# Two attention branches on one core: x in sixteen turned pieces, one run of dummy products, three buffers for a polynomial tile, and a new written-out order

## The chip, the core and the metric

The kernel runs on one core of a Trainium2 chip. The metric is device time in microseconds (us) of one execution; the median of several runs is given. The engines are TensorE (PE, with its weight loads as PEld), ScalarE (ACT), VectorE (DVE), GpSimd (POOL) and SyncE (SP, which here issues most of the transfers).

## The reference

Two branches work on inputs of 2048 rows by 1024 columns, with 32 heads of width 32, in bfloat16. Their results are put side by side.

```python
# branch A: plain attention
qkv = (x @ wqkv).reshape(B, S, 3, H, Dh)
p = softmax(q @ k.T * Dh ** -0.5)
a = (p @ v) @ wo

# branch B: four segments of 512 rows, causal inside a segment, with a memory M, z
for s in range(4):
    p = softmax(qs @ ks.T * scale + mask)
    a_dot = p @ vs
    a_mem = (phi(qs) @ M) / (phi(qs) @ z + 1e-06)
    o = g * a_mem + (1.0 - g) * a_dot        # g = sigmoid(beta)
    M = M + phi(ks).T @ vs
    z = z + phi(ks).sum(over the rows)
b = concat(o) @ wo
return concatenate([a, b], axis=-1)
```

`phi(t)` is `t + 1` where t is positive and `exp(t)` elsewhere.

## The kernel before

**Tiles.** Four heads make a group (eight groups, `g` or `j`). A unit of branch A is one group and 256 queries, a column `c` of eight; a unit of branch B is a pair of groups in one segment. A unit is worked in sets: TensorE forms the logits of 128 keys for four heads ("row products", line 1169), ScalarE takes the exponential of 128 by 1024 of them at a time (line 1262) into a ring `P` of 20 buffers, and TensorE multiplies the result with V (line 1375) and with ones (line 1382), the latter for the sum of the softmax. DVE and POOL normalize (`turned`, line 1489 and on). Projections, output products and the memory of branch B are jobs that run between: eight groups of four products, nearly all issued by one helper (`mm4`, line 808).

**The polynomial.** In every unit of branch A after the first group's split parts, four key tiles send one head's tile around ScalarE: DVE reads the logits into `Y` (line 1210), POOL squares them into `Z` (line 1219) and writes a parabola into `Pc` (line 1220). The rings `Y`, `Z` and `Pc` have 3, 2 and 2 buffers. The exponential and the parabola hold for small logits; a guard computes a bound from squared norms (`square`, `guard_cols`, line 1613, `guard_end`, line 1668) and sets a bias and a flag (lines 1685 and 1693), on which ScalarE branches to a guarded version. A few numbers that the guards leave lie in the small tiles `cols`, `bias`, `braw` and `fp`.

**The head.** Before the first exponentials, branch A's x is loaded and turned on the way, by transposing transfers on SyncE's queue (`turn`, line 1547), in the pieces that `X_PIECES` lists: quarter of the rows, first and last block of 128 columns, and two times for the planner. The weights of group 0 (`W_A`) and half of those for V (`Wv_A`) are issued on ScalarE's own queue, ahead of and around the load of its table (line 1042). TensorE begins with products on a zeroed tile (`warm`, on `sqB`), in three runs of 7, 6 and 3 groups: at the start, behind the first two products of the first quarter, and at that quarter's end. `quarter` forms K and Q of one quarter of the rows; their copies (lines 1761 and 1763) and squares (line 1596) lead to the first two exponentials, which run without a guard, to the first bound (line 1306 makes good what it finds), to six guarded exponentials (line 1240), to the second bound, which rests on the second quarter, and to a correction factor (line 1646).

**The order.** Nothing is scheduled on the chip. A program simulates the engines with costs of its own, spreads the jobs evenly between release and due times (`level`, `plan_jobs`), and writes a fixed queue for each engine (`schedule`). `rearrange` then moves single entries as `MOVES` tells: "12+3" steps 12 on and pulls the entry three places behind to this one. Each engine takes its queue in order and waits on semaphores. `BANKS` says which of two accumulator banks each job or accumulation uses. In `emit`, an instruction of ACT, DVE or POOL that must come after a near one on its own engine is made to wait for it.

Of the kernel before, what the change touches and what calls it, by code (L numbers as in the profile page):

```python
# [6 lines left out]
dt = mybir.dt  # L7
ACT = mybir.ActivationFunctionType
# [18 lines left out]
    "667676677676667666667666766676666666667676677676666676666676666666676766776766676666676666667676766776766667666666767667"  # L27
    "767666766666766667666766677666666667677676767666667666766666666676767667676667666666676676677676666676666766666667766776"
    "766667666667666766667666667666666666766767767676677666666667676776766666766666667677676766676666667676776766676667666766"
    "67666676666666676666766"  # L30
# [3 lines left out]
Y_RING, Z_RING, C_RING = 3, 2, 2  # L34
# [9 lines left out]
CUBIC = [[0, 2, 4, 6], [0, 2, 4, 6], [0, 2, 4, 6], [0, 2, 4, 6], [0, 2, 4, 6], [0, 2, 4, 6], [0, 2, 4, 6], [0, 2, 4, 6], [0, 2, 4, 6], [0, 2, 4, 6], [0, 2, 4, 6], [0, 2, 4, 6], [0, 2, 4, 6], [0, 2, 4, 6], [0, 2, 4, 6], [0, 2, 4, 6]]  # L44
# [9 lines left out]
BIAS_PART = (17, 16, 18)  # L54
PARTS = ((0, 0), (0, 1), (1, 0), (1, 1), (1, 2), (1, 3), (2, 0), (2, 1), (2, 2), (2, 3))
WARM = (7, 6, 3)
X_PIECES = ((0, 0, 2, 0.7, 3.8), (0, 2, 4, 0.7, 5.8), (0, 4, 6, 2.2, 4.5), (0, 6, 8, 2.2, 2.9), (1, 0, 4, 2.6, 3.0),
            (1, 4, 8, 2.5, 3.0), (2, 0, 8, 4.4, 3.5), (3, 0, 8, 4.9, 3.5))
# [85 lines left out]
class Op:  # L144
# [17 lines left out]
    def __hash__(self):  # L162
# [4 lines left out]
SWITCH = 0.10  # L167
AHEAD_OF_GUARD = 2
# [607 lines left out]
class _Kernel:  # L776
# [925 lines left out]
    def plan_prologue(self):  # L1702
# [8 lines left out]
        def warm(key, n, dur, behind=None):  # L1711
            for _ in range(n):
                o = self.pe(lambda e: self.mm4(e, self.ps[:, 512 * 5:512 * 6], dummy[:, 0:P], dummy[:, :], True, True), dur, key,
                            [rd], [self.bank[5]])
                if behind:
                    o.order.add(behind)
# [530 lines left out]
```

## Time and profile before

| | us |
|---|---|
| median of three runs (lowest, highest) | 1068.11 (1067.42, 1068.65) |
| the profiled execution | 1067.08 |
| its span | 1065.3 |
| busy: PE, ACT, POOL, DVE | 1025.6, 1001.1, 723.5, 710.7 |

The span runs from the first to the last instruction of the profiled execution; what lies outside it makes the rest of that execution's own time. Views of the profile give times in us from the span's start, and shapes as partitions by elements. A bracket at the end of a line of the order of time holds the idle time of the engine just before, and what ended it. In a group's line the busy time stands behind the bar, and the idle time before its instructions behind the next.

### The profile page before, as it was taken

What the parts mean: (1) busy time and instruction counts of PE and PEld (TensorE: products, weight loads), DVE (VectorE), ACT (ScalarE), POOL (GpSimd) and SP (SyncE); (2) the same over time, 40 slices, a digit from 0 to 9 for tenths busy, and PEclk for the clock granted to TensorE, in tenths of its full rate; (3) what the DMA queues carried; (4) which work ended last, traced back from release to release, by engine and by line L of the source; (5) the groups of instructions that cost most, each with busy time, mean ns of one, the idle gap of its engine ahead of it and who ended that gap; (6) DMA issues with size and microseconds to landing.
All of it is one profiled execution on the core that took longest, in us unless ns stands there. A gap on an engine that the chain in (4) does not pass through costs nothing.

```text
span 1065.3 us, 55407 instructions
## 1 busy us (share of the span) xinstructions
PE 1025.6 (96%) x25276; PEld 554.2 (52%) x25276; DVE 710.7 (67%) x1452; ACT 1001.1 (94%) x1193; POOL 723.5 (68%) x999
## 2 busy tenths in 40 slices
PE   8999999999999999999999998999999999999998
PEld 4556555566554454556555454466545544445554
DVE  2446677765666878787656888778556887674544
ACT  4999999999999999998999999899999899999996
POOL 1005578667776897888867897897756777885552
PEclk9999999999999999999999999999999999999999
DMA  9013261016121530034321322044131750122101
GB/s 205 17 43 92 67 140 25 15 19 142 30 78 50 134 84 18 3 60 101 89 78 48 76 55 48 10 91 81 38 84 50 194 143 3 37 67 77 33 23 58
DMA packets 171547, 72.01 MB, mean 68 GB/s; under 512 B 135216, under 2 KB 169520, under 8 KB 171312
## 3 DMA queue, kind: packets, MB, share of 16 engines
q1 hardware_dynamic: 167904, 67.40, 26.2%
q8 instruction: 199, 3.26, 1.3%
q10 hardware_dynamic: 3408, 1.05, 0.5%
q14 instruction: 36, 0.29, 0.1%
HBM read 45.23 MB, written 11.67 MB: 53 GB/s over the span
## 4 chain that ended last, share of the span: by engine, by line
PE 60%; ACT 31%; DVE 6%; issue 1%; DMA 1%; POOL 1%; SPq 1%; ACTq 0%; DVEq 0%; POOLq 0%
ACT P L1262 30%; PE ps L808 30%; PE ps L1169 12%; PE ps L1375 9%; PE ps L1382 8%; PE ps L1836 1%; DVE Y L1210 1%; DVE T L1489 1%; DMA xT_A<-in_A_x_dram 1%; DVE KQ_B L1583 1%; SPq L1547 1%; ACT P L1240 0%; DVE PKQ_B L1895 0%; POOL Z L1219 0%; PE ps L1613 0%
## 5 line engine op out<-in xcount | busy, mean ns | idle before, releaser
L1262 ACT ACTIVATE P<-ps 128x1024 bf16<-128x1024 f32 (+1 forms) x1178 | 991.0, 996 | 40.6 <-PE ps L1169 25.1
L1219 POOL TENSOR_TENSOR Z<-Y 128x512 f32<-128x512 f32 x287 | 304.6, 1066 | 202.9 <-DVE Y L1210 181.9
L1382 PE MATMUL ps<-P,onesb 128*32 128x256 bf16 (+1 forms) x4386 | 300.6, 270 | 0.0
L1375 PE MATMUL ps<-P,V_A 128*32 128x256 bf16 x3618 | 256.8, 274 | 0.7 <-DVE V_A L1846 0.3
L1210 DVE TENSOR_SCALAR Y<-ps 128x512 f32<-128x512 f32 x239 | 163.6, 685 | 117.7 <-PE ps L1169 107.1
L1169 PE MATMUL ps<-KQ_A 32*128 32x256 bf16 x4096 | 204.4, 272 | 15.4 <-ACT P L1262 9.5
L1220 POOL TENSOR_SCALAR Pc<-Z 128x512 bf16<-128x512 f32 x239 | 156.2, 657 | 23.1 <-PE ps L1382 6.3
L1169 PEld LDWEIGHTS ps<-KQ_A 32*128 32x128 bf16 x4096 | 62.8, 92 | 168.5 <-ACT P L1262 114.4
L808 PE MATMUL ps<-xT_A,W_A 128*32 128x512 bf16 (+1 forms) x2184 | 142.0, 369 | 3.1 <-DMA xT_A<-in_A_x_dram 2.6
L1382 PEld LDWEIGHTS ps<-P,onesb 128*32 128x32 bf16 x4386 | 128.6, 96 | 27.9 <-issue 11.3
L808 PE MATMUL ps<-xT_B,W_B 128*32 128x512 bf16 (+1 forms) x2160 | 137.8, 370 | 1.5 <-DVE gc L1792 0.6
L1375 PEld LDWEIGHTS ps<-P,V_A 128*32 128x32 bf16 x3618 | 107.7, 96 | 32.8 <-issue 14.7
L1382 PE MATMUL ps<-Pc,onesb 128*32 128x256 bf16 x478 | 123.1, 273 | 0.0
L1375 PE MATMUL ps<-Pc,V_A 128*32 128x256 bf16 x478 | 122.3, 274 | 0.4 <-POOL Pc L1220 0.2
L1291 POOL TENSOR_SCALAR_AFFINE_SELECT P<-P 128x768 bf16<-128x768 bf16 (+1 forms) x96 | 75.3, 800 | 34.6 <-ACT P L1262 33.9
L1489 DVE STREAM_TRANSPOSE T<-ps 128x512 f32<-128x512 f32 x122 | 86.6, 710 | 16.2 <-PE ps L1382 12.6
L808 PEld LDWEIGHTS ps<-xT_A,W_A 128*32 128x32 bf16 x2184 | 52.4, 96 | 49.1 <-issue 18.9
L808 PEld LDWEIGHTS ps<-xT_B,W_B 128*32 128x32 bf16 x2160 | 51.6, 96 | 46.5 <-issue 19.3
L808 PE MATMUL ps<-Wo_B,OT_B 128*32 128x512 bf16 (+1 forms) x1072 | 71.6, 371 | 0.1
L808 PE MATMUL ps<-Wv_B,xT_B 128*32 128x512 bf16 (+1 forms) x1076 | 68.8, 371 | 0.1
L1583 DVE CAST KQ_A<-ps 128x512 bf16<-128x512 f32 x60 | 41.1, 685 | 37.7 <-PE ps L808 37.0
L1583 DVE CAST outsb<-ps 128x512 bf16<-128x512 f32 x56 | 38.7, 690 | 33.2 <-PE ps L1375 17.1
(107 smaller groups left out, 1207.6 us busy)
## 6 DMA issues: line engine op xcount, KB each, us to landing
Wv_B<-in_B_wv_dram SPq DMA_DIRECT2D x32, 256.0 KB, 3.7
W_B<-in_B_wk_dram SPq DMA_DIRECT2D x32, 256.0 KB, 3.8
W_B<-in_B_wq_dram SPq DMA_DIRECT2D x32, 256.0 KB, 4.3
Wo_B<-in_B_wo_dram SPq DMA_DIRECT2D x32, 256.0 KB, 3.2
out_dram<-outsb SPq DMA_DIRECT2D x56, 128.0 KB, 1.9
W_A<-in_A_wqkv_dram SPq DMA_DIRECT2D x14, 256.0 KB, 4.3
ot_a_scratch<-OTst SPq DMA_DIRECT2D x50, 64.0 KB, 1.8
xT_A<-ot_a_scratch SPq DMA_DIRECT2D x6, 512.0 KB, 4.6
```

What stands on the lines that cost most here:

```text
L808: ins = e.matmul(out[r], w[:, r], x, start=start, stop=stop, tile_position=(0, 32 * t), skip_group_check=True)
L1169: ins = e.matmul(out, kap, qap, start=st, stop=True, tile_position=(32 * h, 0), skip_group_check=True)
L1210: o = self.dve(lambda e: e.tensor_scalar(Y[:, :], src, SCALE, MID, ALU.mult, ALU.add), 512, key - 9.0, [self.bank[bank]], [rY], fixed=0.15)
L1219: self.pool(lambda e: e.tensor_tensor(Z[:, :], Y[:, :], Y[:, :], ALU.mult), 512, key, [rY], [rZ], rate=0.58)
L1220: return self.pool(lambda e: e.tensor_scalar(dst, Z[:, :], C2, REST, ALU.mult, ALU.add), 512, key, [rZ], [rP], rate=TS_RATE)
L1262: a = self.act(guarded if early and not free else lambda e: e.activation(dst, src, ACT.Exp, scale=SCALE), cols, key, rd, wr, fixed=EXP_FIXED)
L1291: self.pool(lambda e: e.affine_select(v, v, pattern=pat, compare_op=ALU.is_ge, fill=0.0, base=0, channel_multiplier=-1), 2 * nd * P, key + ...
L1375: ins = e.matmul(self.ps[32 * h:32 * h + 32, 512 * obk + q0:512 * obk + q0 + nq], v, p, start=first, stop=last, tile_position=(0, 32 * h), ...
L1382: ins = e.matmul(self.ps[32 * h:32 * h + 32, lcol + q0:lcol + q0 + nq], self.onesb[:, 0:32], p, start=False, stop=last, tile_position=(0, ...
L1489: self.dve(lambda e: e.transpose(T2[:, :], src), 512, k - NORM_K, [obk.res], [ro, rl], fixed=0.17)
L1547: return self.dma(lambda e: e.dma_start(dst, src, transpose=True), sem, key, reads, writes, issue=issue, lat=lat, gate=gate)
L1583: self.dve(lambda e: e.tensor_copy(dst, src), 512, key, [self.at(b)], rdst, fixed=0.155)
```

## The change

- `X_PIECES` holds 16 pieces of 512 rows and 256 columns, in place of four such pieces, two of 512 columns and two of 1024. `quarter` takes the columns in steps of two blocks for K and Q in turn, in both quarters. Half of `Wv_A` is issued behind the landing of the third piece (before: the second), the other half after the twelfth (before: after the seventh, at the same place in x).
- `WARM` is 14: one run of dummy products at the start, and none later.
- `emit` no longer makes an instruction wait for a transfer that its own queue issued just before. That concerns the table load, which stood behind the landing of `W_A`.
- `Pc` has three buffers. `cols`, `bias` and `braw` are packed, and `fp` lies in `braw`.
- `MOVES` is replaced as a whole (entries for PE 2717, now 2838; ACT 20, 42; DVE 1140, 1215; POOL 704, 779; the strings are left out below), `BANKS` in some places. `POLYS` and `ROOM` are new tables; with the values that they hold here, every unit has the key tiles that it had, and the job times are not stretched.

```diff
-Y_RING, Z_RING, C_RING = 3, 2, 2
+Y_RING, Z_RING, C_RING = 3, 2, 3
-CUBIC = [[0, 2, 4, 6], [0, 2, 4, 6],
...
+POLYS = "4444444444444444444444444444444444444444444444444444444444444444"
+CUBIC = {"3": (0, 2, 4), "4": (0, 2, 4, 6), "5": (0, 1, 2, 4, 6)}
-BIAS_PART = (17, 16, 18)
+BIAS_PART = (7, 6, 8)
-WARM = (7, 6, 3)
-X_PIECES = ((0, 0, 2, 0.7, 3.8), (0, 2, 4, 0.7, 5.8), (0, 4, 6, 2.2, 4.5), (0, 6, 8, 2.2, 2.9), (1, 0, 4, 2.6, 3.0),
-            (1, 4, 8, 2.5, 3.0), (2, 0, 8, 4.4, 3.5), (3, 0, 8, 4.9, 3.5))
+WARM = 14
+X_PIECES = tuple((n // 4, n % 4 * 2, n % 4 * 2 + 2, 0.95, lat) for n, lat in enumerate((5.5, 5.2, 5.5, 5.6, 6.4) + (6.3,) * 11))
+ROOM_W = 36.0
+ROOM = (0.0,) * 27
...
-                o.deps |= {x for x in o.order if x.eng == e and n - x.pos <= 12 and not (o.prog and x.prog)}
+                o.deps |= {x for x in o.order if x.eng == e and n - x.pos <= 12 and x.sem is None and not (o.prog and x.prog)}
...
-        self.cols = sb("cols", [P, 64], dt.float32)
+        self.cols = sb("cols", [P, 32], dt.float32)
-        self.bias = sb("bias", [P, 64], dt.float32)
+        self.bias = sb("bias", [P, 12], dt.float32)
-        self.braw = sb("braw", [P, 2], dt.float32)
+        self.braw = sb("braw", [P, 4], dt.float32)
-        self.fp = sb("fp", [P, 2], dt.float32)
+        self.fp = self.braw[:, 2:4]
...
-        return CUBIC[n // 4 % len(CUBIC)]
+        return CUBIC[POLYS[n]]
...
-        self.item(-99.5, lambda key: warm(key, WARM[0], 0.38))
+        self.item(-99.5, lambda key: warm(key, WARM, 0.38))
...
-                if n == 1:
+                if n == 2:
                     self.load_WAv(0, key, 0, 1, "ACT").deps.update(rs[0].w)
-                elif n == 6:
+                elif n == 11:
                     self.load_WAv(0, key, 1, 2)
...
-            cut = (0, 4, 8) if c else (0, 4, 6, 8)
-            for i, kq in [(i, kq) for lo, hi in zip(cut, cut[1:]) for kq in range(2) for i in range(lo, hi)]:
+            for i, kq in [(i, kq) for lo in range(0, 8, 2) for kq in range(2) for i in range(lo, lo + 2)]:
...
-                    if not c and not kq and i == 1:
-                        warm(key, WARM[1], 0.2165, o)
-                        for w in self.pg.ops[-WARM[1]:]:
-                            w.order.add(o)
-                        held = self.pg.ops[-1]
-                    if not c and not kq and i == 2:
-                        o.order.add(held)
             self.last_quarter = o
-            if not c:
-                warm(key, WARM[2], 0.2165, o)
...
-        self.loads = level(jobs, -1e9, 1e9)
+        self.loads = level([(at(r), at(d), c, f) for r, d, c, f in jobs], -1e9, 1e9)
         for (r, d, c, f), (t, v) in zip(jobs, self.loads):
+            t = real(t)
             self.item(t, lambda key, d=d, f=f: self.with_due(d, f, key))
```

`at` and `real` map a time to a stretched one and back, with one factor for each 36 us of the plan (`ROOM`); all factors are 0.

More of the change, by code (lines that the diff above doesn't have):

```diff
@@ L26 @@
     "666767676767666767766766676667666766676666676666766676666676767767666667666667676767676666766666766676766776766676666766"
[L27 to L30, printed above, removed]
+    "667676677676667666667666766676666666667676677676666676666676667666776766776766676666676667666676766776766667666666767667"
+    "767666766666766667666766676666666667667676767666667666766666766676767667676667666666676676677676666676666766666667766776"
+    "766667666667666766667666667667667666766767767666677666666667676776766666767666667677676766676666667676776766676667666766"
+    "67666676666666676666767"
 )
@@ L43 @@
 FREE_B = 0.5 * 32 ** -0.5 * FREE * FREE
-CUBIC = [[0, 2, 4, 6], [0, 2, 4, 6], [0, 2, 4, 6], [0, 2, 4, 6], [0, 2, 4, 6], [0, 2, 4, 6], [0, 2, 4, 6], [0, 2, 4, 6], [0, 2, 4, 6], [0, 2, 4, 6], [0, 2, 4, 6], [0, 2, 4, 6], [0, 2, 4, 6], [0, 2, 4, 6], [0, 2, 4, 6], [0, 2, 4, 6]]
+POLYS = "4444444444444444444444444444444444444444444444444444444444444444"
+CUBIC = {"3": (0, 2, 4), "4": (0, 2, 4, 6), "5": (0, 1, 2, 4, 6)}
 TS_RATE = 1.085
@@ L198 @@
     "PE": (
[95 rows of a table removed]
[99 rows of a table added]
     ),
     "ACT": (
-        "14+4 21+1 1+1 1+1 1+1 1+1 1+1 1+1 1+1 1+1 1+1 1+1 1+1 1+1 1+1 1+1 1+1 1+1 1+1 1142+1 "
+        "12+3 21+1 1+1 1+1 1+1 1+1 1+1 1+1 1+1 1+1 1+1 1+1 1+1 1+1 1+1 1+1 1+1 1+1 1+1 1+1 1+1 52+1 1+1 1+1 1+1 1+1 1+1 1+1 1+1 "
+        "1+1 1+1 1+1 1+1 1+1 1+1 1+1 1+1 1+1 1+1 1+1 1+1 1071+1 "
     ),
     "DVE": (
[39 rows of a table removed]
[41 rows of a table added]
     ),
     "POOL": (
[24 rows of a table removed]
[26 rows of a table added]
     ),
@@ L1214, in plan_cube @@
         self.item(T + 0.001, f)
-        return (lambda e: e.activation(dst, Y[:, :], ACT.Exp, bias=self.bias[:, 60 + bc:61 + bc], scale=1.0), bc, rY, rP, last, t)
+        return (lambda e: e.activation(dst, Y[:, :], ACT.Exp, bias=self.bias[:, 10 + bc:11 + bc], scale=1.0), bc, rY, rP, last, t)
     def parabola(self, Y, Z, dst, rY, rZ, rP, key):
@@ L1672, in guard_end @@
         m = n * nper
-        ci = 16 + 8 * (self.nge % 4)
+        ci = 16 + 4 * (self.nge % 4)
         self.nge += 1
@@ L1688, in guard_end @@
             if bc < 2:
-                self.dve(lambda e, bc=bc: e.tensor_scalar(self.bias[:, 60 + bc:61 + bc], self.bias[:, bc:bc + 1], -MID, None, ALU.add), 1,
+                self.dve(lambda e, bc=bc: e.tensor_scalar(self.bias[:, 10 + bc:11 + bc], self.bias[:, bc:bc + 1], -MID, None, ALU.add), 1,
                          key + 0.4, [rb], [self.r_biasr[bc]])
@@ L1709, in plan_prologue, with warm @@
         dummy, rd = self.sq["B"][0], self.r_sq["B"][0]
-        def warm(key, n, dur, behind=None):
+        def warm(key, n, dur):
             for _ in range(n):
[L1713 to L1716, printed above, removed]
+                self.pe(lambda e: self.mm4(e, self.ps[:, 512 * 5:512 * 6], dummy[:, 0:P], dummy[:, :], True, True), dur, key,
+                        [rd], [self.bank[5]])
         self.item(-99.6, lambda key: self.dve(lambda e: e.memset(dummy[:, :], 0.0), 512, key, (), [rd]))
         self.item(-99.4, lambda key: self.dve(lambda e: e.memset(self.flags[:, 0:1], 0), 1, key, (), [self.r_flags]))
-        self.item(-99.5, lambda key: warm(key, WARM[0], 0.38))
+        self.item(-99.5, lambda key: warm(key, WARM, 0.38))
         def loads(key):
@@ L2186, in plan_jobs, with real_in @@
                     self.item(self.T_end + 5.0 + (0, 2, 1, 3)[k], lambda key, row=row, hf=hf, p=p, k=k: self.job_last(row, hf, p, allb[k], key, "ACT" if k < 2 else "DVE"))
-        self.loads = level(jobs, -1e9, 1e9)
+        at = lambda t: t + sum(x * min(max(t - ROOM_W * n, 0.0), ROOM_W) for n, x in enumerate(ROOM))
+        real = lambda u: u - sum(x * ROOM_W for x in ROOM) if u >= knots[-1] else real_in(u)
+        def real_in(u):
+            n = bisect.bisect_right(knots, u) - 1
+            return u if n < 0 else ROOM_W * n + (u - knots[n]) / (1.0 + ROOM[n])
+        knots = [at(ROOM_W * n) for n in range(len(ROOM) + 1)]
+        self.loads = level([(at(r), at(d), c, f) for r, d, c, f in jobs], -1e9, 1e9)
         for (r, d, c, f), (t, v) in zip(jobs, self.loads):
+            t = real(t)
             self.item(t, lambda key, d=d, f=f: self.with_due(d, f, key))
```

324 rows, old and new, of the table MOVES are left out of this document.

## The prediction

> **What bounds the kernel now.** The page comes first: the engines' totals, the chain that ended last, and the costliest group.
>
> ```profile
> span 1065.3 us, 55407 instructions
> PE 1025.6 (96%) x25276; PEld 554.2 (52%) x25276; DVE 710.7 (67%) x1452; ACT 1001.1 (94%) x1193; POOL 723.5 (68%) x999
> PE 60%; ACT 31%; DVE 6%; issue 1%; DMA 1%; POOL 1%; SPq 1%; ACTq 0%; DVEq 0%; POOLq 0%
> L1262 ACT ACTIVATE P<-ps 128x1024 bf16<-128x1024 f32 (+1 forms) x1178 | 991.0, 996 | 40.6 <-PE ps L1169 25.1
> ```
>
> Two engines are nearly full, and the chain passes between them: 60% TensorE, 31% ScalarE. ScalarE is idle for 64.2 us (1065.3 less 1001.1), of which 40.6 lie ahead of the exponentials of L1262. No work of the two engines is taken out in quantity, so the change can only close such gaps or open new ones. They lie at the head and in a few stretches of the body. First the head, on ScalarE and then on TensorE (order of time).
>
> ```profile
> 6.33 1.28 ACT L1042 ACT_TABLE_LOAD   x1 [6.33 <-DMA W_A<-in_A_wqkv_dram]
> 7.07 0.37 ACTq L1524 DMA_DIRECT2D Wv_A<-in_A_wqkv_dram  x1
> ...
> 14.37 1.94 ACT L1262 ACTIVATE P<-ps 128x1024 bf16<-128x1024 f32 x2 [0.59 <-PE ps L1169]
> 17.44 0.20 ACT L1306 ACTIVATE warm<-warm 128x1 f32<-128x1 f32 x1 [1.14 <-DVE bias L1685]
> 18.19 6.14 ACT L1240 ACTIVATE P<-ps,bias 128x1024 bf16<-128x1024 f32 x6 [0.55 <-PE ps L1169]
> 25.14 0.29 ACT L1646 ACTIVATE fp<-bias 128x1 f32<-128x1 f32 x1 [0.81 <-DVE bias L1685]
> 25.60 20.27 ACT L1262 ACTIVATE P<-ps 128x1024 bf16<-128x1024 f32 x22 [0.17 <-issue]
> ```
> ```profile
> 1.25 2.96 PE L808 MATMUL ps<-sqB 128*32 128x512 bf16 x28 [1.25 <-DVE sqB L1717]
> 6.51 0.62 PE L808 MATMUL ps<-xT_A,W_A 128*32 128x512 bf16 x8 [2.30 <-DMA xT_A<-in_A_x_dram]
> 6.94 2.49 PE L808 MATMUL ps<-sqB 128*32 128x512 bf16 x24
> 9.18 3.96 PE L808 MATMUL ps<-xT_A,W_A 128*32 128x512 bf16 x56
> ...
> 14.62 0.40 PE L808 MATMUL ps<-xT_A,W_A 128*32 128x512 bf16 x4 [0.30 <-DMA xT_A<-in_A_x_dram]
> 14.85 0.40 PE L1613 MATMUL ps<-sqA,blk 128*32 128x128 bf16 x16
> ```
>
> ScalarE begins its exponentials at 14.37, has two of them, waits for the first bound (17.44), does six, waits for the second bound (25.14), and is full from 25.60 on. TensorE decides this: dummy products on `sqB`, 2.30 us of waiting for the first piece of x, two real products of four instructions each, then six more dummies in the middle of the first quarter, which ends only at 13.14 (9.18+3.96). The clock that was granted explains the slow middle (per window: length, then busy us and instructions of PE, PEld, DVE, ACT and POOL, then the granted clock, the DMA share and GB/s):
>
> ```profile
> 3.85:7.27 3.42, 1.12 (x24) 0.50 (x20) 0.00 (x0) 0.94 (x1) 0.00 (x0) 1.00 1.30 261
> 7.27:10.68 3.41, 3.41 (x40) 1.60 (x35) 0.00 (x0) 0.55 (x2) 1.96 (x12) 0.50 1.24 174
> 17.50:26.00 8.50, 7.56 (x167) 4.55 (x164) 4.47 (x14) 6.98 (x9) 0.00 (x0) 1.00 1.16 242
> ```
>
> A window in which TensorE worked 1.12 us of 3.42 is followed by one at half clock (0.50). Half a clock doubles a product: 2.96/7 = 0.42 us for one of four instructions in the cold run at 1.25, against 3.70/17 = 0.218 us in this piece of the chain:
>
> ```profile
> 1056.19 3.70 PE ps L808 x68
> ```
>
> The pieces of x (SyncE's queue, and two stretches that hold one issue each, the third piece and the fourth):
>
> ```profile
> 0.80 17.73 SPq L1547 DMA_TRANSPOSE xT_A<-in_A_x_dram  x7
> ```
> ```profile
> 19.21 5.08 SPq L1547 DMA_TRANSPOSE xT_A<-in_A_x_dram  x1
> ```
> ```profile
> 3.93 1.84 SPq L1547
> 5.81 1.30 SPq L1547
> ...
> 7.15 7.42 DMA xT_A<-in_A_x_dram
> ```
> ```profile
> DMA to landing us min/median/max: 4.4/4.4/4.4
> ```
> ```profile
> DMA to landing us min/median/max: 4.0/4.0/4.0
> ```
>
> So the third piece lands at 3.93+4.4 = 8.33, the fourth at 5.81+4.0 = 9.81, and the fifth, twice as large, at 7.15+7.42 = 14.57. The first quarter had all its data at 9.81 and finished 3.3 us later.
>
> **The change part by part.** *One run of 14 dummies.* Started at 1.25 as now, they pass 6.1 products by 3.85 at 0.42 us, and the other 7.9 at 0.218 take 1.7 us: done at 5.6, ahead of the first x at 6.51. The nine dummies behind it are gone. The window from 3.85 then holds 1.7 us of dummies and 0.76 of x, 2.5 of 3.42 instead of 1.12, and I take the next window to be at full clock.
>
> The first four pieces are cut as now, so they land as now, and the quarter takes its four products per piece as they land: 6.51 to 7.38, to 8.25, 8.33 to 9.2, 9.81 to 10.68, or 10.86 with a last instruction's 0.40 us instead of 0.218. That is 2.28 us ahead of 13.14. If the window were cold all the same, the products behind 7.38 would run at 0.42: 9.1, 10.7, and the last four warm to 11.6; 1.4 us would be left.
>
> The Trainium skill, "TensorE: Matmul & The Clock Gate", Part 1 (The HAM clock gate), says that the activity window is 3413 ns and free-running, not reset when a kernel starts. The windows of this trace agree in length (3.42 and 3.41); no run here shows another phase yet. By that rule the gain is not the same in every execution; the rival "phase" below works out, from the rows above, an execution of the old kernel without a cold window.
>
> *Sixteen pieces.* Behind the first quarter stands the guard product (L1613), which sets ScalarE's second start. The squares it reads are done at 14.23:
>
> ```profile
> 13.47 0.76 DVE L1596 TENSOR_TENSOR sqA<-KQ_A 128x512 bf16<-128x512 bf16 x2
> ```
>
> It begins 0.6 later, at 14.85, behind a product that waited for the fifth piece (14.57). With the quarter 2.28 earlier the squares are done at 11.95. The fifth piece has half the bytes now and lands between 7.15+4.0 = 11.15 and, if it is no faster than the large one, 14.57. I take the middle, 12.9, and find the guard at 13.1 or earlier: a gain of 1.75 to 2.9, in the best case the 2.28 and the 0.6 together; in the worst (14.57) none. I take 2.3 for the head. The second bound, 25.14, hangs on x that landed long before and on TensorE's order, so it can move up by the same.
>
> On SyncE's queue the first four issues took 6.31 us (0.80 to 7.11), 1.58 each. Sixteen would end at 26, with 0.6 for a weight piece among them at 26.7, against 24.29 now (19.21+5.08). What is behind, weights of group 1 and the last x, would land up to 2.4 later. The second half of x is first read here:
>
> ```profile
> 27.56 0.94 PE L808 MATMUL ps<-xT_A,W_A 128*32 128x512 bf16 x16
> ```
>
> With the head 2.3 shorter that is 25.3, and only the second quarter's pieces are needed by then, so I cost it at nothing; uncovered, it would cost those 2.4 us once. The Trainium skill, "DMA: Bandwidth & Descriptors", section Bandwidth, speaks against this cut: batch DMAs to 1 MiB or more; by it, the rival "cut" below would hold. Here it is not borne out: where only pieces of 256 KB were under way (3.85 to 7.27) the rate was 261 GB/s, with 1 MB pieces (17.50 on) 242.
>
> *ScalarE's queue.* The table load no longer waits for the weights (6.33). ScalarE's copy comes after 10.9, so this hides. The issue of `Wv_A` now waits for the third piece, 8.33 instead of 7.07. If the table load is queued behind it, that is 8.33+0.37+1.28, ready at 10.0, still 0.9 ahead of the copy; without that cover the cost is at most 1.28. Smaller column and bias arrays move no time: the instructions stay.
>
> *The ring of three, and the moves.* The waits of ScalarE, and those of GpSimd ahead of the tile that gets a third buffer:
>
> ```profile
> ACT P L1262 <- PE ps L1169: 25.1, 47, 2.0
> ```
> ```profile
>   PE ps L1382: 6.3, 21
>   PE ps L1375: 4.8, 19
>   PE ps L808: 4.6, 27
> ```
>
> A third `Pc` removes up to 6.3+4.8+4.6 = 15.7 us of waiting on an engine that is 68% full; on the chain POOL has 1%. By itself I give it nothing, between 0 and the chain's 1% (10 us). The moves (TensorE's list goes from 2717 to 2838 entries, DVE's from 1140 to 1215) replace the whole order, and no row shows the new one. Bounds come from stretches of the old:
>
> ```profile
> 266.30:319.60 53.30, 52.94 (x1304) 27.36 (x1300) 33.65 (x68) 53.26 (x65) 37.83 (x52) 1.00 0.19 54
> 639.20:692.40 53.20, 48.83 (x1188) 25.12 (x1180) 42.41 (x90) 47.95 (x57) 43.66 (x65) 1.00 0.14 29
> 799.00:852.20 53.20, 51.82 (x1264) 27.50 (x1264) 40.57 (x83) 47.96 (x57) 38.47 (x52) 1.00 0.45 122
> ```
>
> ScalarE idles 0.04 us in the tightest of these and 5.25 and 5.24 in the two loosest. If those became as tight, 10.4 us would go; if two tight ones became as loose, 10.4 would come. I take a gain of 2.6, a quarter of it, ring included: in both loose stretches neither engine is full (TensorE idles 4.4 and 1.4), so there a better order exists, while elsewhere one of the two is already near its limit.
>
> The sum: the profiled execution took 1067.08 (span 1065.28). Less 2.3 and 2.6 it is 1062.2. The median of the three timed runs, 1068.11, is 1.03 above it, so the forecast for a median is 1063.2.
>
> **The rivals.** *Phase, and an order that is no better.* Without a cold window the old first quarter would run from 6.94 with 6 dummies and 14 products at 0.218, ending at 11.3, 11.5 with the last instruction's rest. The new one ends at 10.86, so the head's gain is 0.6. With nothing from the body: 1068.11 - 0.6 = 1067.5. For it: a half-empty window could fall otherwise, and the median lies a microsecond above the profiled run. Against: the profiled run has the cold window and 2.30 us of waiting in front of it.
>
> *Row products come later (the slower side).* TensorE takes its queue in order. Where the new order puts one more projection group ahead of the row products (L1169), the exponential behind waits, and that costs 25.1/47 = 0.53 us each time. Five more such waits than the old order has cancel the head, nine make the change slower by over 0.2%; with eighteen (one in some 60 us) it is 9.5 - 2.3 = 7.2 slower, 1075.3. For it: two of three stretches above show what an order with such gaps looks like, and the sums on both engines are too near the span to absorb a wait. Against: stretches such as 266.30:319.60 are there already, with room to do the same elsewhere.
>
> *Cut: sixteen pieces bring nothing at the guard.* If the queue of 16 is served no faster, the fifth piece lands at 14.57 again, the guard waits as before, and the head gives 0; with the body's 2.6 the time is 1065.5. For it: the DMA share stands above 1 in each of the windows shown. Against: 174 GB/s in 7.27:10.68, so the engines were not delivering all they can.
>
> **How the numbers follow.** Forecast 0.64, phase with no better order 0.13, late row products 0.17, cut without use 0.06. A difference of 0.2%, 2.1 us, is about what a measurement of this kernel tells from none. The forecast and the useless cut are faster by more than that (0.70), phase is within it (0.13), late products slower (0.17). The forecast's own range is 1055 to 1066: the head's 2.9 with 10.4 from the body gives 1054.8, the head's 1.4 with a body of 0.7 gives 1066. The range to hold 8 in 10 adds the rival within 0.2% and the mild end of the late products: 1055 to 1070.5.
>
> **What would show it.** In the new profile: dummies in one run to 5.6 and none later; every window from 3.85 on at full clock; the first exponential at about 12.1 instead of 14.37, the second start near 15 instead of 17.44, the full run from about 23.3 instead of 25.60. In the body: ScalarE's wait for L1169 below 25.1, and the stretches around 640 to 692 and 799 to 852 with under 4 us of idle ScalarE. I am wrong in the head if a window behind 7.27 is cold or the guard still starts after 14; wrong in the body if that wait grows beyond 30 us.

## The result, and the profile after

| | before | after |
|---|---|---|
| median of four runs (lowest, highest), us | 1068.03 (1067.42, 1068.65) | 1062.21 (1061.23, 1062.53) |
| ratio, 95% interval | | 0.9944 [0.9927, 0.9961] |
| profiled execution, us | 1067.08 | 1062.53 |

The change is 5.8 us faster; the forecast was 4.9 us faster, 1063.2. That the sum came out is luck: by the profile its term for the head was off by 3.2 us to one side and its term for the body by 2.1 us to the other. First the page: the engines, the chain that ended last, and the group of the exponentials.

```profile
span 1060.8 us, 55089 instructions
PE 1024.7 (97%) x25160; PEld 549.4 (52%) x25160; DVE 711.4 (67%) x1452; ACT 1001.4 (94%) x1193; POOL 726.7 (69%) x999
PE 69%; ACT 21%; DVE 5%; POOL 2%; issue 1%; SPq 1%; DMA 1%; ACTq 0%; DVEq 0%; POOLq 0%
```

The work is what it was (TensorE 1024.7 against 1025.6, ScalarE 1001.4 against 1001.1); only idle time went. What ScalarE waits for, the largest causes (total us, times, longest):

```profile
ACT P L1273 <- PE ps L1180: 17.8, 35, 2.5
ACT P L1273 <- PE ps L1393: 11.2, 15, 2.0
...
ACT warm L1317 <- DVE bias L1696: 3.8, 1, 3.8
```

L1273 and L1180 are the old L1262 and L1169: the wait for row products fell from 25.1 to 17.8. The wait of the first bound (L1317, before L1306) rose from 1.14 to 3.8, so the head did not gain. ScalarE and then TensorE in order of time:

```profile
13.18 1.94 ACT L1273 ACTIVATE P<-ps 128x1024 bf16<-128x1024 f32 x2 [0.59 <-PE ps L1180]
18.90 0.20 ACT L1317 ACTIVATE warm<-warm 128x1 f32<-128x1 f32 x1 [3.78 <-DVE bias L1696]
20.33 4.13 ACT L1251 ACTIVATE P<-ps,bias 128x1024 bf16<-128x1024 f32 x4 [1.23 <-PE ps L1180]
...
26.51 1.05 ACT L1273 ACTIVATE P<-ps 128x1024 bf16<-128x1024 f32 x1
```
```profile
1.28 5.80 PE L819 MATMUL ps<-sqB 128*32 128x512 bf16 x56 [1.28 <-DVE sqB L1726]
6.91 2.76 PE L819 MATMUL ps<-xT_A,W_A 128*32 128x512 bf16 x48
10.89 1.05 PE L819 MATMUL ps<-xT_A,W_A 128*32 128x512 bf16 x16 [1.23 <-DMA xT_A<-in_A_x_dram]
...
13.61 0.66 PE L1624 MATMUL ps<-sqA,blk 128*32 128x128 bf16 x16
14.04 2.79 PE L819 MATMUL ps<-xT_A,W_A 128*32 128x512 bf16 x24
16.60 0.28 PE L1679 MATMUL ps<-sel,dg 128*32 128x64 bf16 x4
```

The first exponential starts 1.19 earlier (13.18, was 14.37), the guarded ones 2.14 later (20.33, was 18.19), and the full run 0.91 later (26.51, was 25.60). Two windows of TensorE's clock say why the products behind 14.04 are slow: a window with 1.56 us of work, in which TensorE had waited for the fourth piece and for the copies, is followed by one at half clock. In the old kernel that window lay in the first quarter; it has moved behind it.

```profile
10.00:13.40 3.40, 1.56 (x28) 0.60 (x30) 1.45 (x3) 0.81 (x2) 0.00 (x0) 1.00 1.09 202
13.40:16.82 3.42, 3.42 (x52) 1.78 (x52) 0.45 (x2) 1.72 (x2) 0.00 (x0) 0.50 1.05 206
```

So the 4.4 us by which the last exponential starts earlier (1049.16, was 1053.51) came from behind the head: exponential 40 (counted from 0) starts at 55.64 (was 55.30), and from there to the last one the kernel takes 993.52 where it took 998.21. The gain is spread: exponential by exponential, there are steps such as these, before the change, each a ScalarE start with its idle time:

```profile
89.32 2.43 ACT L1262 ACTIVATE P<-ps 128x1024 bf16<-128x1024 f32 x3 [1.50 <-PE ps L1668]
```
```profile
486.14 1.94 ACT L1262 ACTIVATE P<-ps 128x1024 bf16<-128x1024 f32 x2 [1.47 <-PE ps L1169]
```
```profile
889.59 1.94 ACT L1262 ACTIVATE P<-ps 128x1024 bf16<-128x1024 f32 x2 [1.54 <-PE ps L1169]
```

In each of them TensorE has other products ahead of those that ScalarE waits for: 32 of L1836 and 32 of PV (the products with V) and sums before the guard's spread (L1668, the products of `sel` and `dg`), which ends at 89.32, for instance. From the start of the exponential before to the start of this one it was 2.51, 2.51 and 2.58 us; after the change it is 0.99, 1.65 and 0.90, of which the exponential itself takes 0.9. Other places lose: exponential 948 comes 1.79 us later behind its forerunner than before the change. What is left is the sum of both: the new kernel is 0.36 us behind at exponential 70, and ahead by 1.81 at 100, 1.60 at 460, 3.88 at 700 and 4.35 at the last. The GpSimd tile with a third buffer has lost the waits for TensorE that were 6.3, 4.8 and 4.6; what its engine waits for ahead of it is now:

```profile
  issue: 14.9, 71
  POOL Pc L1231: 0.8, 4
  POOL Z L1230: 0.6, 3
  ACT P L1273: 0.5, 1
```

### The profile page after: what moved, and what is told of

It is laid out like the page before. It is cut to its first block, busy times and chain, and to the rows that moved or that the text cites. A ratio compares the mean times of both kernels' runs of the same rounds, so it can differ in the third digit from the quotient of the medians.

```text
span 1060.8 us, 55089 instructions
## 1 busy us (share of the span) xinstructions
PE 1024.7 (97%) x25160; PEld 549.4 (52%) x25160; DVE 711.4 (67%) x1452; ACT 1001.4 (94%) x1193; POOL 726.7 (69%) x999
## 4 chain that ended last, share of the span: by engine, by line
PE 69%; ACT 21%; DVE 5%; POOL 2%; issue 1%; SPq 1%; DMA 1%; ACTq 0%; DVEq 0%; POOLq 0%
PE ps L819 34%; ACT P L1273 21%; PE ps L1180 14%; PE ps L1386 10%; PE ps L1393 9%; POOL Z L1230 1%; DVE Y L1221 1%; PE ps L1835 1%; DVE T L1500 1%; PE ps L1624 1%; SPq L1558 1%; DMA xT_A<-in_A_x_dram 1%; POOL Pc L1231 0%; DVE OT_B L1917 0%; DVE sqB L1607 0%
## 5 line engine op out<-in xcount | busy, mean ns | idle before, releaser
L1273 ACT ACTIVATE P<-ps 128x1024 bf16<-128x1024 f32 (+1 forms) x1178 | 991.6, 988 | 34.6 <-PE ps L1180 17.8
L1180 PE MATMUL ps<-KQ_A 32*128 32x256 bf16 x4096 | 203.6, 272 | 13.6 <-ACT P L1273 6.4
L1231 POOL TENSOR_SCALAR Pc<-Z 128x512 bf16<-128x512 f32 x239 | 156.4, 660 | 10.4
L1180 PEld LDWEIGHTS ps<-KQ_A 32*128 32x128 bf16 x4096 | 62.4, 92 | 168.0 <-ACT P L1273 116.5
L1594 DVE CAST KQ_B<-ps 128x512 bf16<-128x512 f32 x64 | 44.1, 689 | 28.1 <-PE ps L819 27.5
```

Source lines behind the costliest of these rows:

```text
L1180: ins = e.matmul(out, kap, qap, start=st, stop=True, tile_position=(32 * h, 0), skip_group_check=True)
L1231: return self.pool(lambda e: e.tensor_scalar(dst, Z[:, :], C2, REST, ALU.mult, ALU.add), 512, key, [rZ], [rP], rate=TS_RATE)
L1273: a = self.act(guarded if early and not free else lambda e: e.activation(dst, src, ACT.Exp, scale=SCALE), cols, key, rd, wr, fixed=EXP_FIXED)
L1594: self.dve(lambda e: e.tensor_copy(dst, src), 512, key, [self.at(b)], rdst, fixed=0.155)
```

## The experiments

One table for all, since most readings rest on it. "Body" is the time from the start of exponential 40 to that of the last one, so that it holds nothing of the head. "Stops" are idle times of TensorE of 0.3 us and more with no semaphore behind them, told at the end. Both come from the one profiled execution, the median from all runs, the ratio against the kernel before on the same chip.

| kernel | median us | ratio, 95% interval | exponential 8 | body | stops | body less stops |
|---|---|---|---|---|---|---|
| before | 1068.03 | | 25.60 | 998.21 | 0.33 | 997.9 |
| after | 1062.21 | 0.9944 [0.9927, 0.9961] | 26.51 | 993.52 | 1.84 | 991.7 |
| old head, new body | 1061.65 | 0.994 [0.9927, 0.9953] | 25.35 | 992.58 | 0.47 | 992.1 |
| new head, old body | 1067.69 | 0.9993 [0.9984, 1.0003] | 26.10 | 997.78 | 0 | 997.8 |
| old with ring of three | 1066.74 | 0.9983 [0.9974, 0.9991] | 27.32 | 997.83 | 0.62 | 997.2 |
| new with ring of two | 1072.76 | 1.0037 [1.0024, 1.005] | 25.67 | 1005.15 | 2.87 | 1002.3 |
| new order to 300 us, then old | 1066.65 | 0.9988 [0.9979, 0.9998] | 28.29 | 997.59 | 1.83 | 995.8 |
| old pieces, one run of dummies | 1064.79 | 0.9967 [0.9954, 0.998] | 26.45 | 996.35 | 4.47 | 991.9 |
| late dummies | 1063.76 | 0.9958 [0.9943, 0.9973] | 26.20 | 995.47 | 3.49 | 992.0 |
| mended head | 1062.14 | 0.9945 [0.9932, 0.9958] | 23.72 | 995.19 | 2.59 | 992.6 |
| mended head, large pieces | 1062.99 | 0.9947 [0.9934, 0.9959] | 23.65 | 993.75 | 2.64 | 991.1 |
| mended head, weights ahead | 1063.99 | 0.996 [0.9945, 0.9974] | 23.49 | 993.33 | 2.35 | 991.0 |
| new with large pieces | 1062.86 | 0.9939 [0.9926, 0.9952] | 26.41 | 995.58 | 3.27 | 992.3 |
| new with small loads | 1060.03 | 0.9921 [0.9907, 0.9935] | 28.16 | 991.75 | 0.93 | 990.8 |

### Head or body

Old head, new body: pieces, dummies and the order of the plan's first 29 us as before the change; the rest new.

```diff
-WARM = 14
+WARM = (7, 6, 3)
-X_PIECES = tuple((n // 4, n % 4 * 2, n % 4 * 2 + 2, 0.95, lat) for n, lat in enumerate((5.5, 5.2, 5.5, 5.6, 6.4) + (6.3,) * 11))
+X_PIECES = ((0, 0, 2, 0.7, 3.8), (0, 2, 4, 0.7, 5.8), (0, 4, 6, 2.2, 4.5), (0, 6, 8, 2.2, 2.9), (1, 0, 4, 2.6, 3.0),
...
```

> The old head (eight pieces of x, dummies in runs of 7, 6 and 3, the old order up to about 29 us) with the new order and the ring of three behind it. Theory one (the gain is the new order of the body; the new head gave nothing and in the profiled execution lost 0.9 us at the ninth exponential, 26.51 against 25.60): about 1061.3, not slower than the changed kernel. Theory two (the prediction's split, 2.3 us from the head and the rest from the body): about 1064.5.

New head, old body, the counterpart: the changed kernel with the old `MOVES` and `BANKS` behind those 29 us.

> The new head (sixteen pieces, one run of 14 dummies, the new order up to about 29 us) with the old order behind it; the ring has three buffers. Theory one: about 1068.9, no faster than before. Theory two: about 1065.7.

They part cleanly: with the new body 1061.65, with the old one 1067.69, whose interval holds 1. Both have the ring of three. Within the noise the whole gain is the body's, and ScalarE's wait for row products goes with it: 17.5 us with the new body, 24.3 with the old one. No window at half clock is in the second kernel's records, and it gained nothing by that.

### Ring or order

```diff
 old with ring of three (on the kernel before)
-Y_RING, Z_RING, C_RING = 3, 2, 2
+Y_RING, Z_RING, C_RING = 3, 2, 3
...
```

The packed tiles and the table load that waits for nothing (it starts at 1.90, in the kernel before at 6.33) come with it; the order of the queues is the old one.

> The kernel before, with its own head and its own order, and only the third buffer for the polynomial tile. Theory one in its plain form (the order alone): 1068, within 1 us. Theory three (the third buffer removes waits by itself, whatever the order): 1064 to 1066, with the waits of GpSimd ahead of the tile (15.7 us) gone.

```diff
 new with ring of two (on the changed kernel)
-Y_RING, Z_RING, C_RING = 3, 2, 3
+Y_RING, Z_RING, C_RING = 3, 2, 2
```

> The changed kernel with two buffers for the polynomial tile and its own order otherwise. If the order alone carries the gain: 1062 to 1063. If the order rests on the third buffer: 1065 to 1069, with GpSimd waiting for TensorE's products ahead of the tile and TensorE for the tile, on the chain.

In the old order the third buffer takes GpSimd's waits away and gives 0.17% of the median, 0.7 us of the profile's body. In the new order it is worth 10.6 us of body (1002.3 against 991.7): with two buffers the new order is slower than the old kernel, by 0.37%. GpSimd's idle time ahead of `Pc` in that run, and then who waited for `Pc`:

```profile
  PE ps L1412: 15.5, 27
  issue: 15.1, 72
  PE ps L1419: 7.6, 19
...
  PEld ps L1412: 3.3, 9
  PE ps L1412: 1.5, 4
```

L1412 and L1419 are PV and sums. As I read it, the new order uses `Pc` later; a buffer then comes free later, GpSimd is behind, and TensorE waits 4.8 us for it. In the old order it was 1.2 and 0.2. ScalarE waits 28.2 us for row products there, 10.4 more than with three buffers, which is about the whole 10.6; the steps from the one wait to the other were not followed. So order and ring are one edit: neither is worth anything near 6 us alone.

New order to 300 us, then old: `MOVES` and `BANKS` of the changed kernel for what the plan starts before 300, the old ones behind, three buffers.

> The changed kernel's head and order up to about 300 us, the old order behind, ring of three. If the gain was made in separate stretches (the trace shows 2.2 us between the 70th and the 100th exponential, nothing from there to the 460th, the rest behind): 1.8 to 2.2 us below the kernel with the new head and the old body (0.9993 of the kernel before), so a ratio near 0.9975. If a gain in one stretch is given back by the old order behind it: a ratio of 0.999 or more.

Body less stops is 995.8, between the two others: 2.0 less than with the old order throughout (997.8, the new head with the old body), 4.1 more than with the new one (991.7). The kernels with the old order lie between 997.2 and 997.9, those with the new one and three buffers that do the whole work between 991.0 and 992.6. By the profiles, then, the gain is not in one place; both parts hold some of it. The medians do not show it: the ratio is 0.9988, neither the 0.9975 nor the 0.999 or more that was expected, and its interval overlaps that of the new head with the old body.

### The head

Old pieces, one run of dummies: the old eight pieces, the old order of the head and the new single run of 14, with the new body.

```diff
-X_PIECES = tuple((n // 4, n % 4 * 2, n % 4 * 2 + 2, 0.95, lat) for n, lat in enumerate((5.5, 5.2, 5.5, 5.6, 6.4) + (6.3,) * 11))
+X_PIECES = ((0, 0, 2, 0.7, 3.8), (0, 2, 4, 0.7, 5.8), (0, 4, 6, 2.2, 4.5), (0, 6, 8, 2.2, 2.9), (1, 0, 4, 2.6, 3.0),
...
```

> The old eight pieces of x with one run of 14 dummies (and the quarter in steps of two blocks), the old order of the head without its other dummies, the new order behind. The prediction's step: the first quarter ends near 10.9 and the first exponential starts near 12.1 if the clock stays full. If the later dummies were what held the clock: a window at half clock follows the quarter, as in the changed kernel, and the second start (the third exponential) stays behind 18. Median 1061.5 to 1063.

The first exponential starts at 12.39, near the 12.1 of the forecast and 0.79 us ahead of the changed kernel's, since the fourth piece is there earlier:

```profile
10.11 1.05 PE L860 MATMUL ps<-xT_A,W_A 128*32 128x512 bf16 x16 [0.89 <-DMA xT_A<-in_A_x_dram]
```

In the four profiles with eight pieces the fourth lands at 9.29 to 10.06, in the ten with more pieces at 10.85 to 11.71. The fifth lands at 14.18 to 15.11 and at 12.18 to 13.86. So the cut, with the issue of `Wv_A` that moves with it, brings the fifth piece earlier and the fourth later. Exponential 8 starts at 26.45, as with sixteen pieces (26.51), with the half clock at 14.85 to 18.26 here. The body less stops is that of the other new orders. The median is 2.6 us longer than the changed kernel's and above the 1063 expected; the profile has 2.6 us of stops more, but its execution is the longest of the five (1066.36), so this does not explain the median. Whether the cut gains anything stays open.

Late dummies: on the changed kernel, four groups ahead of the fourth piece's products and four behind the first quarter.

```diff
+                    if not c and not kq and i == 6:
+                        warm(key, 4, 0.2165)
...
             self.last_quarter = o
+            if not c:
+                warm(key, 4, 0.2165)
```

> The changed kernel with four more dummy products ahead of the fourth piece's products and four behind the first quarter, where TensorE stood idle (1.23 and 0.79 us). If the missing dummies cost the head its clock: no window at half clock between 7 and 20 us whatever the phase, the ninth exponential at about 25.5 instead of 26.51, and a median about 1 us lower, 1061.2. If TensorE's full queue behind the head sets the time: the head is shorter but the median stays at 1062.2.

No half-clock window was left, and exponential 8 gained 0.31 (26.20). So the clock was not what held the second start; the next kernel shows that the order was. The median, 1063.76, is above both that were expected, with 3.49 us of stops in the profile (1064.17). Mended head: late dummies, and in `MOVES` the guard's products and bias, the first products with `Wv_A` and the row products of the first four sets put ahead of the second quarter's later pieces; the correction factor later; pieces planned at the issue times measured.

```diff
-X_PIECES = tuple((n // 4, n % 4 * 2, n % 4 * 2 + 2, 0.95, lat) for n, lat in enumerate((5.5, 5.2, 5.5, 5.6, 6.4) + (6.3,) * 11))
+X_PIECES = tuple((n // 4, n % 4 * 2, n % 4 * 2 + 2, 1.3, lat) for n, lat in enumerate((4.9, 4.2, 4.7, 5.4, 6.4, 5.9, 5.7, 5.9) + (6.0,) * 8))
...
```

> As the one with late dummies, and in addition the guard's two products, the bias on DVE and the row products of the first four sets stand earlier in their queues, ahead of products that wait for pieces six to eight; the planner's times for the pieces of x are those measured. Head time carries to the end: third exponential at about 17 instead of 20.33, ninth at about 23.7 instead of 26.51, median 1059.5. TensorE's work behind the head sets the time: the ninth exponential is as early, but by the seventeenth the lead is under 1 us and the median is 1061 to 1062.

Now the second start is early and the full run begins 2.8 us ahead of the changed kernel's (23.72):

```profile
17.32 6.14 ACT L1300 ACTIVATE P<-ps,bias 128x1024 bf16<-128x1024 f32 x6 [0.74 <-PE ps L1229]
```

By exponential 20 the lead is gone, and the median is 1062.14, not 1059.5. SyncE's queue and TensorE in that run:

```profile
21.47 7.20 SPq L1607 DMA_TRANSPOSE xT_A<-in_A_x_dram  x4
28.71 1.23 SPq L1578 DMA_DIRECT2D W_A<-in_A_wqkv_dram  x2
```
```profile
34.18 1.05 PE L868 MATMUL ps<-xT_A,W_A 128*32 128x512 bf16 x16 [1.38 <-DMA W_A<-in_A_wqkv_dram]
```

The weights of group 1 stand behind sixteen issues. Three kernels follow: ten pieces with the mended head, the same with the weights ahead of the last piece, and ten pieces with the changed kernel's own order.

```diff
-X_PIECES = tuple((n // 4, n % 4 * 2, n % 4 * 2 + 2, 1.3, lat) for n, lat in enumerate((4.9, 4.2, 4.7, 5.4, 6.4, 5.9, 5.7, 5.9) + (6.0,) * 8))
+X_PIECES = tuple((n // 4, n % 4 * 2, n % 4 * 2 + 2, 1.3, lat) for n, lat in enumerate((4.9, 4.2, 4.7, 5.4, 6.4, 5.9, 5.7, 5.9))) + ((2, 0, 8, 4.5, 4.5), (3, 0, 8, 4.5, 4.5))
...
-                elif n == 11:
+                elif n == 8:
```

> The mended head with the last two quarters of x in one transfer each, as before the change, in place of four each: ten issues in front of the weights of group 1 instead of sixteen. In the run with the mended head the weights were issued at 28.71 and landed at 34.13, and TensorE waited 1.4 and 1.7 us for them. Theory (the queue of x takes the head's lead back): eight small issues of 1.3 to 1.6 us, two large of 4.2 and half of the weights for V put the issue at 22 to 23 and the landing at 28 to 29; both waits go, exponential 18 keeps some 2.5 of the 2.8 us that exponential 8 is ahead of the changed kernel, and the time is 1059.5. Rival (TensorE's full queue takes it back): the lead shrinks to under 0.5 by exponential 40 although the weights land by 29, and the time is 1062.

> As the one above, but the weights of group 1 are issued ahead of the last quarter of x. Theory: they land at 24 to 25, x ends at 29 or 30 instead of 27; both are early enough, so the time is the same as above within 0.5 (1059.5). Rival: the last quarter of x is read early, TensorE waits for it at some 28 to 30 and 1 to 2 us of the lead are lost: 1061.

> The changed kernel with the last two quarters of x in one transfer each; its order is as it was. Theory (there the late weights are hidden, since its head is 2.8 us later): the weights are issued 3 to 4 us earlier than at 26.74 and nothing follows from it: 1062.2, within 0.5. Rival (the sixteen issues already cost the changed kernel): a wait for the weights shrinks and the time is 1060.5 to 1061.

With ten pieces the weights are issued at 25.57 (not at 22 to 23) and the wait for them is gone, but of the lead only 1.24 is left at exponential 40: TensorE's queue takes back 1.2 between exponentials 8 and 12 already, where ScalarE waits 1.02 for row products. That is neither the theory's 2.5 nor the rival's 0.5, and the theory's 1059.5 was not reached (1062.99). With the weights ahead, the last quarter of x is late, which was the rival of that run, and TensorE waits longer than before:

```profile
31.24 0.72 PE L868 MATMUL ps<-xT_A,W_A 128*32 128x512 bf16 x12 [2.56 <-DMA xT_A<-in_A_x_dram]
```

For the changed kernel itself ten pieces in place of sixteen do nothing (1062.86, as against 1062.21; the exponentials from 8 to 40 are 0.11 earlier, and the weights are issued only 1.2 earlier, at 25.55). No kernel here that does the whole work is faster than the changed one by a measurable amount; what is won at the start is less than what one execution differs from the next (1060.07 to 1069.55 with the weights ahead).

### The stops

The exponentials of kernels that share the order of the body drift apart in steps of 0.4 to 1.8 us, at 165 to 167, 248 to 262, 476 to 495, 531 to 533 and 820 to 867 us. At all of them but one TensorE stands still between two products of the same line. The changed kernel at 820, a window ahead of it (DMA share and GB/s last), and the queues from 817.9 to 818.4:

```profile
819.54 0.27 PE L1386 MATMUL ps<-Pc,V_A 128*32 128x256 bf16 x1
820.93 0.29 PE L1386 MATMUL ps<-P,V_A 128*32 128x256 bf16 x3 [1.12 <-issue]
```
```profile
814.00:818.20 4.20, 4.20 (x104) 2.27 (x100) 4.04 (x6) 4.20 (x7) 2.73 (x3) 1.00 1.03 250
```
```profile
q1 hardware_dynamic: 395, 0.11, 131.1%
q8 instruction: 1, 0.02, 16.2%
```

The queue named "instruction" moves packets of 16 KB, 198 in this execution. One began at 818.16 and landed at 819.45; the one before had begun 8.50 us earlier, the next began 3.92 later. In the thirteen profiles of this study ahead of the last run there are 31 stops of 0.4 us or more, and each ends 1.2 to 1.7 us after such a packet has landed. The packets begin 5.3 us apart at the median, so by chance about one stop in ten would end in such a half microsecond (an estimate from these two figures). To see whether bursts of transfers delay them, the last kernel cuts bytes and leaves everything else; its results are not the reference's, as it works with older values in the tiles that are not loaded:

```diff
+        n = 1 if s or j > 1 else 8
-        self.dma(lambda e: e.dma_start(self.WB[sl][:, kq, :, :], src), self.sm_WB[sl][kq], key, [], [self.r_WB[sl][kq]],
+        self.dma(lambda e: e.dma_start(self.WB[sl][:, kq, :n, :], src[:, :n, :]), self.sm_WB[sl][kq], key, [], [self.r_WB[sl][kq]],
...
-        self.dma(lambda e: e.dma_start(self.xT[:, j, :], self.OTd[j, :, :]), self.sm_xT[j], key, self.r_OTd[j], self.r_xT[j],
+        self.dma(lambda e: e.dma_start(self.xT[:, j, :256], self.OTd[j, :, :256]), self.sm_xT[j], key, self.r_OTd[j], self.r_xT[j],
```

> The changed kernel, in its own order, with the same transfers but fewer bytes in four kinds of them behind the head: one block of eight of W_B (from the third group of the first segment on), 64 of 512 columns of Wv_B (all but the first half of the first segment), one block of two of branch B's x (from the second segment on), and 256 of 2048 columns of the reloaded OT rows; what isn't loaded is left out of the computation, the tiles keep older values. In the runs so far TensorE stood still for 0.4 to 1.8 us in the middle of a group of products, with no semaphore to wait for: two such stops in the profile of the changed kernel (0.72 at 249 and 1.12 at 820 us), none to five in the others, and each ended 1.2 to 1.7 us after a packet of 16 KB on the queue of instructions had landed, a packet that began later after the one before than its neighbours did. Theory (the packets of instructions stand behind bursts of transfers): without the bursts no stop of over 0.4 us is left between 150 and 870 us, and the time falls by about what the stops cost, 1.8 of the profile: 1060.4, between 1059.5 and 1061. Rival (the stops come from something else, say which products follow one another): one to four stops of over 0.4 us remain at 249, 480, 530 or 820 to 870 us, and the time is 1061.5 to 1063.

One stop is left where the rival had one to four and the theory none. It lies behind transfers that had not been cut, the weights of branch A, four of them issued from 524.01 to 526.4:

```profile
524.50:529.00 4.50, 4.50 (x116) 2.34 (x112) 2.09 (x4) 4.50 (x7) 2.98 (x5) 1.00 0.94 217
```
```profile
531.43 0.29 PE L1393 MATMUL ps<-P,onesb 128*32 128x256 bf16 x2 [0.93 <-issue]
```

The packet before that stop began 8.86 us after its forerunner and landed at 530.15. Where the bytes were cut, no stop of 0.3 us is left; the share of the transfers in 814 to 822 is 0.39 there, 0.83 in the changed kernel. The median is 1060.03, within the theory's 1059.5 to 1061; the profiled execution, whose head has two windows at half clock (exponential 8 at 28.16), is the longest of the five (1062.43). The profiles say the same of all 32 stops: in the 6 us ahead of the packet the DMA share is 0.72 at the median, ahead of the 2373 other packets between 100 and 1000 us it is 0.15. So bursts make a stop likelier. That they are the cause of each is not shown: one profile with one stop is no proof, for the old head with the new body, with all its bytes, had one too (0.47). The interval of the ratio overlaps the changed kernel's, and ahead of the packet before the stop at 495 in the mended head there was no such burst:

```profile
486.90:492.90 6.00, 5.78 (x180) 3.81 (x176) 4.14 (x7) 5.41 (x8) 5.68 (x7) 1.00 0.37 77
```

By which path a packet is held up, no run here shows.

## Why the prediction was right in sum and wrong in its parts

Two errors cancelled, and the median moved by 5.8 us where the profiled execution moved by 4.55.

**Head, forecast -2.3, measured +0.9.** Three steps failed. The first four pieces did not "land as now": with smaller pieces behind it the fourth landed 1.0 later than taken (10.85, not 9.81), and the dummies were done at 7.08, not 5.6, since the clock stayed low until 6.58; the first exponential came at 13.18 instead of 12.1. Next, "every window from 3.85 on at full clock": I looked at the window with the dummies only, and not at the one behind the quarter, where the old kernel had dummies (the run of three) and the new one has none; 10.00:13.40 had 1.56 us of work. And the step that weighed most: I let the second start move with the guard product ("14.85" to "13.1 or earlier", measured 13.61), as if the order between it and the exponentials stayed. In the new order the spread (16.60) stands behind products of the second quarter, which wait for their pieces, and on DVE the bias that ScalarE waits for stands behind that quarter's copy:

```profile
17.44 0.16 DVE L1704 SCALAR_TENSOR_TENSOR flags<-braw,flags 128x1 int32<-128x1 f32 x1
18.04 0.69 DVE L1760 CAST KQ_A<-ps 128x512 bf16<-128x512 f32 x1 [0.45 <-PE ps L819]
18.65 0.15 DVE L1696 SCALAR_TENSOR_TENSOR bias<-braw 128x1 f32<-128x1 f32 x1
```

The mended head shows that the order decides: with the same pieces the instruction that waits for the bound starts at 16.37 (18.90 in the changed kernel), and the full run starts at 23.72, 23.3 having been forecast. With the dummies alone it was 26.20.

**Body, forecast -2.6, measured -4.7, and -6.2 less stops.** The term was a quarter of a bound taken from the two loosest stretches. Those did not become tighter. Windows of the changed kernel over nearly the same stretches:

```profile
636.50:689.50 53.00, 48.60 (x1168) 24.77 (x1164) 44.32 (x90) 47.75 (x56) 43.38 (x63) 1.00 0.22 40
795.60:848.60 53.00, 50.40 (x1196) 25.84 (x1188) 38.49 (x79) 45.60 (x55) 35.75 (x48) 1.00 0.43 114
```

ScalarE idles 5.25 and 7.40 us in them (forecast: under 4), against 5.25 and 5.24; the stop of 1.12 at 820 lies in the second. The gain came from steps elsewhere, such as the three rows above, less the steps that lose. The sign stood on ScalarE's wait for row products, forecast below 25.1 and measured at 17.8; the size was a guess, and it fell short. What in the new order makes the single steps was not worked out.

**Ring, valued at nothing.** By itself, in the old order, that was right to within the 0.17% measured. But I priced it apart from the order; the new order without it loses 10.6 us of body.

**Queues.** Sixteen issues were forecast to end at about 26.7, with the weights behind; these were issued at 26.74 and nothing waited, as costed. The 2.4 us that I named for the uncovered case came due as soon as the head was shorter: 1.38 on TensorE in the mended head.

**The rivals.** "Phase": the old head met another phase in the run with the ring of three, where the records put the half clock at 14.97 to 18.39; its first quarter ended at 11.43, the rival's 11.5. Its full run began at 27.32 even so: the fifth piece landed at 15.11, and the half clock lay on the guard's products behind it. The Trainium skill, "TensorE: Matmul & The Clock Gate", Part 1, has the window free-running; the traces agree, for windows of 3.41 and 3.42 us begin at different times in every profile, and exponential 8 of the same head order starts anywhere from 25.67 to 28.29 (new with ring of two, new order to 300 us). "Late row products" did not happen with three buffers; with two, something like it did (28.2 us in 48 waits), by another cause. "Cut" was right that the head gains nothing, but not in its reason: the fifth piece did land earlier, and the product that needs it starts at 13.29, not at 14.62.

## What to carry to other kernels

When a written-out order is replaced, each start must be followed through the new order, not through the old one with its times shifted. A deeper ring and the order that uses it are one edit: price them together, by running each without the other. Before a difference of one or two microseconds between two orders is explained, look for stops of the engine within a group that no semaphore explains, and compare times without them.

## What the runs showed of the hardware that was not expected

- TensorE, 97% busy, stopped 32 times for 0.4 to 1.8 us in fourteen profiles (with a shorter one up to 4.47 us in one execution), each time until 1.2 to 1.7 us after the landing of a 16 KB packet of instructions. That packet had begun 4.7 to 8.9 us after the one before, and the next began 3.6 to 5.3 behind it. The interval alone does not make a stop: 5.3 is the median of all, and in the changed kernel 7.97 went by without one (the packet at 648.0). The Trainium skill, "Runtime: NRT & Kernel Launch", section Instruction fetch mechanics, says that instructions are refilled in blocks of 16 KiB while the engine works, mostly hidden; the packets agree (16,384 bytes), "mostly" here means all but 0 to 5 of 198.
- A window of 3.41 us in the head in which TensorE worked 0.91 to 1.39 us was followed by half clock in all seven profiles that have one; with 1.56 it was (after), with 1.47 it was not (new head, old body), and with 1.65 it was not (ring of three, 4.73 to 8.15). Twice the half clock lasted two windows (11.95 to 18.77 in the last run, 12.42 to 19.25 in the new order to 300 us), though TensorE worked 2.63 of 3.41 us in the first of them.
- Four turned pieces of 256 KB took SyncE's queue 7.20 us (21.47, above), one of 1 MB 4.60 to 6.85 in the runs with large pieces: a quarter of the issues, but little less time.
